# Half 1's convolution with one chunk on TensorE and two on VectorE, later casts for half 2, and block 2's loads behind a gate

## The chip, the cores and the metric

The kernel runs on one core of a Trainium2 chip. The metric is the device time of one execution in microseconds. The kernel before takes 698.72 us (median of three runs, 698.67 to 698.84); its profiled execution has a span of 696.4 us.

## The reference

The input x has 8 sequences of 4096 positions and 192 channels. A causal convolution of 7 taps runs along each sequence; the taps are a softmax over a small weight table, one row for each of 8 heads of 24 channels. Its output goes through two matrix products with a leaky ReLU between them. Cut to what matters:

```python
w = softmax(weight, axis=-1)                      # 8 heads x 7 taps
x_pad = concatenate([zeros(6), x], axis=1)
y[b, s, h, :] = sum_k w[h, k] * x_pad[b, s + k, h, :]
h = y.reshape(32768, 192) @ w_in                  # 192 x 2048
g = maximum(0.01 * h, h)
out = g @ w_out                                   # 2048 x 192, float32
```

## The kernel before

**Tiling.** The 192 channels are cut in three chunks of 64 (NCH, CH). Two sequences are handled together, one on each half of the 128 partitions; four such pairs of 4096 positions make 32 blocks of 512 positions. The first five blocks are handled as two halves of 256 positions each, the others whole. A half or a whole block is a "group"; group 0 is half 0 (block 0, first half), group 1 half 1, group 2 half 2 (block 1, first half), group 4 the first half of block 2. For the first two blocks the text also counts quarters of input q = 0 to 3, one for each of groups 0 to 3.

**Way of the data.** For the first two blocks x is loaded in float32 by SyncE (load_first), cast to bf16 (cast_first, line 128), transposed by TensorE into two PSUM tiles "ptr" (transpose_first, line 143) and copied into xt (evac_first, line 157). From block 2 on, GpSimd loads x with the cast in the transfer (load_x, line 79) and SyncE transposes it by DMA (transpose_x, line 94). The convolution reads xt and writes yt. On VectorE a chunk is seven operations (conv_jobs, one of line 176 and six of line 182). In the opening, some chunks are done on TensorE instead, as 28 matmuls with diagonal weights in a high and a low part (pe_conv_jobs, line 201), whose sum "acc" in PSUM is scaled into yt (line 207, or line 317 on ScalarE).

**The two products.** A step mm1 computes 12 (for a half) or 6 (for a whole block) matmuls into a "ph" tile and one ScalarE activation that writes g (lines 356 and 363). The second product is cut in slots: slot q does one matmul of output q // 16 on the upper 64 rows and, LAG = 24 slots later, one on the lower 64 rows (line 376). An output is copied out of PSUM when its last lower matmul is done (evac_o, line 415), and every second one starts a store (line 418). Half 0 has no slots, as nothing is ready yet; in half 1 there are 16 slots after each of its four pairs of steps.

**Order.** Everything is issued in the written order on each engine; semaphores follow from the tiles. The main loop goes over groups i, pairs of steps j, and steps u. While group i is in the products, VectorE does the convolution of group i + 1 (the list "ahead", handed out in portions after each j). Two PSUM pools matter: "ph" with two tiles of two banks, and "po" with four slots that serve the second product's outputs, the transposed tiles "ptr" (two at a time) and "acc". A slot is free when the last reader of its tile is done.

**The opening.** TensorE runs a few dummy matmuls on zeros (warm) between its first real ones. Half 0's convolution does chunks 0 and 1 on TensorE (NPEC = 2) and chunk 2 on VectorE. In half 0's loop (i == 0), after u = 1, quarter 1 is transposed and evacuated; half 1's convolution does chunk 2 on VectorE, chunk 0 on TensorE after u = 3 and chunk 1 after u = 5. Quarter 2 is cast by ScalarE after u = 2, transposed after u = 4 and evacuated at j = 3, after which VectorE does four of half 2's 21 operations before the rest of them in half 1's loop. Quarter 3 is cast in half 1's loop after u = 0 and u = 2, transposed after j = 1, and evacuated after j = 3, behind the remaining operations of half 2. Block 2's loads and DMA transposes (lines 333 and 334) are issued ahead of the main loop.

Of the kernel before, what the change touches and what calls it, by code (L numbers as in the profile page):

```python
# [9 lines left out]
FP32 = mybir.dt.float32  # L10
# [4 lines left out]
def kernel(  # L15
# [54 lines left out]
    def load_x(blk):  # L70

        if blk >= NBLK:
            return
        rp, st = divmod(blk, NB)
        t = xb_pool.tile([128, NCH, SUB, 2, CH], BF16, name="x_bf")
        src = x[:, st * ST : (st + 1) * ST, :].rearrange("r (s p) d -> r p s d", p=128)
        for c in range(NCH):
            for e in range(2):
                nc.gpsimd.dma_start(  # L79
                    out=t[:, c, :, e, :],  # L80
                    in_=src[2 * rp + e, :, :, c * CH : (c + 1) * CH],
                )
        x_bf[blk] = t

    def transpose_x(blk):

        if blk >= NBLK:
            return
        rp, st = divmod(blk, NB)
        if st == 0:  # L90
            new_xt(rp)
        t = x_bf.pop(blk)
        for c in range(NCH):
            nc.sync.dma_start_transpose(
                out=xt[rp][:, c, HALO + st * ST : HALO + (st + 1) * ST].rearrange(
                    "p (s k) -> p s k", s=SUB
                ),
                in_=t[:, c, :, :, :].rearrange("p s e k -> p (s e k)"),
            )
# [24 lines left out]
    def cast_first(q, e, copy):  # L124
        if q % 2 == 0 and e == 0:
            x_bf[q // 2] = xb_pool.tile([128, NCH, SUB, 2, CH], BF16, name="x_bf")
        h = q % 2
        copy(  # L128
            out=x_bf[q // 2][:, :, h * HS : (h + 1) * HS, e, :],
            in_=x_nat[q][:, e, :, :].rearrange("p s (c k) -> p c s k", c=NCH),  # L130
        )
# [3 lines left out]
    def transpose_first(q):  # L135
        ts = [
            psum_o.tile([128, HS, NCH, CH], BF16, name=f"ptr{i}", tag="po") for i in range(2)
        ]
        for s in range(HS):
            for c in range(NCH):  # L140
                for i in range(2):
                    ps = slice(i * CH, (i + 1) * CH)
                    nc.tensor.transpose(  # L143
                        out=ts[i][:, s, c, :],
                        in_=x_bf[q // 2][ps, c, (q % 2) * HS + s, :, :].rearrange(
                            "p e k -> p (e k)"
                        ),
                        identity=ident[ps, ps],
                    )
        ptr[q] = ts  # L150
# [11 lines left out]
    def conv_jobs(grp, chunks=range(NCH)):  # L162
        blk, t0, T = grp
        rp, st = divmod(blk, NB)
        if blk not in yt:
            yt[blk] = yt_pool.tile([128, NCH, ST], BF16, name="yt")
        y = yt[blk]
        jobs = []
        for c in chunks:
            for k in range(K):  # L170
                a = BASE + k + st * ST + t0
                src = xt[rp][:, c, a : a + T]
                dst = y[:, c, t0 : t0 + T]
                if k == 0:
                    jobs.append(
                        lambda s=src, d=dst, c=c: nc.vector.tensor_scalar_mul(  # L176
                            d, s, wk[:, c, 0:1]
                        )
                    )
                else:  # L180
                    jobs.append(
                        lambda s=src, d=dst, c=c, k=k: nc.vector.scalar_tensor_tensor(  # L182
                            out=d, in0=s, scalar=wk[:, c, k : k + 1], in1=d,
                            op0=mybir.AluOpType.mult, op1=mybir.AluOpType.add,
                        )
                    )
        return jobs

    def pe_conv_jobs(grp, c):


        blk, t0, T = grp
        acc = psum_o.tile([128, ST], FP32, name="acc", tag="po")
        jobs = []
        for p in range(2):
            for k in range(K):
                a = BASE + k + blk * ST + t0
                for e in range(2):
                    ps = slice(e * CH, (e + 1) * CH)
                    jobs.append(  # L200
                        lambda k=k, p=p, a=a, e=e, ps=ps: nc.tensor.matmul(  # L201
                            out=acc[ps, :T], lhsT=diag[c][ps, p, k, :],
                            rhs=xt[0][ps, c, a : a + T],
                            start=(k == 0 and p == 0), stop=(k == K - 1 and p == 1),
                        )
                    )
        return jobs, lambda scale: scale(yt[blk][:, c, t0 : t0 + T], acc[:, :T], rsum[:, c, :])
# [40 lines left out]
    def warm(n):  # L248
        for _ in range(n):
            nc.tensor.matmul(  # L250
                out=wa[:, 0, 0:HT], lhsT=zero[:, 0:128], rhs=zero, start=True, stop=True
            )
# [9 lines left out]
        out=w9[:, 0:K], in_=w9[:, 0:K], func=mybir.ActivationFunctionType.Exp,  # L262
        bias=nmax, scale=1.0, accum_out=w9[:, K : K + 1],
    )
    warm(7)
    wps = psum_h.tile([128, 2, ST], FP32, name="wps", tag="ph")
    for c in range(NCH):
        nc.tensor.matmul(  # L268
# [7 lines left out]
    cast_first(0, 1, nc.scalar.copy)  # L276

    wraw = wps[:, 0, 0 : NCH * (K + 1)].rearrange("p (c k) -> p c k", c=NCH)
    wkh = const_pool.tile([128, NCH, K], BF16, name="wkh")
    wkl = const_pool.tile([128, NCH, K], FP32, name="wkl")  # L280
    nc.vector.tensor_copy(out=wkh, in_=wraw[:, :, 0:K])
    nc.vector.tensor_sub(wkl, wraw[:, :, 0:K], wkh)


    diag = [const_pool.tile([128, 2, K, CH], BF16, name=f"diag{c}") for c in range(NPEC)]
# [14 lines left out]
        return act  # L300

    transpose_first(0)
    warm(3)
    diag_high(0)
    diag_low(0, range(2))
    evac_first(0, nc.vector.tensor_copy, nc.scalar.copy)
# [23 lines left out]
    cast_first(1, 0, nc.vector.tensor_copy)  # L330
    cast_first(1, 1, nc.vector.tensor_copy)
    load_first(3)
    load_x(2)
    transpose_x(2)


    g, po, osb, seal = {}, {}, {}, {}
# [70 lines left out]
    def evac_o(n):  # L408
# [7 lines left out]
        if n % 2 == 1:  # L416
# [3 lines left out]
                in_=osb.pop(n // 2),  # L420
            )

    slot, avail = 0, 0
    for i, grp in enumerate(groups):
        blk, t0, T = grp
        steps = T // 64
        if t0 == 0:
            g[blk] = g_pool.tile([128, NFC, 2, ST], BF16, name="g", tag="g")
        quota = (avail - slot) // steps

        if i == 0:
            ahead, pe_ahead = [], []
        elif i == 1:
            ahead = early[4:]
        else:
            ahead = conv_jobs(groups[i + 1]) if i + 1 < len(groups) else []
        per = -(-len(ahead) // (steps - 1)) if T == ST else -(-len(ahead) // steps)
        for j in range(steps):
            for u in range(2 * j, 2 * j + 2):
                mm1(grp, u)  # L440
                if i == 0 and u == 1:
                    transpose_first(1)
                    evac_first(1, nc.vector.tensor_copy, nc.vector.tensor_copy)
                    ahead = conv_jobs(groups[1], range(NPEC, NCH))
                    evacs = []
                    for c in range(NPEC):
                        pe_jobs, evac_y = pe_conv_jobs(groups[1], c)
                        pe_ahead += pe_jobs
                        evacs.append(evac_y)
                    per = len(ahead)  # L450
                if i == 0 and u == 2:
                    for e in range(2):
                        cast_first(2, e, nc.scalar.copy)
                if i == 0 and u == 4:
                    transpose_first(2)
                    evacs[0](act_scale)
                if i == 0 and u in (3, 5):
                    for job in pe_ahead[: 4 * K]:
                        job()
                    pe_ahead = pe_ahead[4 * K :]  # L460
                if i == 1 and u in (0, 2):
                    cast_first(3, u // 2, nc.scalar.copy)
            for _ in range(quota):
                mm2_slot(slot)
                slot += 1
            if i == 0 and j == 3:
                evac_first(2, nc.vector.tensor_copy, nc.vector.tensor_copy)
                early = conv_jobs(groups[2])
                for job in early[:4]:
                    job()  # L470
                evacs[1](nc.vector.tensor_scalar_mul)
            for job in ahead[per * j : per * (j + 1)]:
                job()
            if i == 1 and j == 1:
                transpose_first(3)
            if i == 1 and j == 3:
                evac_first(3, nc.vector.tensor_copy, nc.vector.tensor_copy)

            last_half = t0 + T == ST
            if j == steps // 4 and last_half:  # L480
                load_x(blk + 3)
            if j == steps // 2 and last_half and blk > 0:
                transpose_x(blk + 2)
        avail += 2 * T // 128 * NFC
# [37 lines left out]
```

## Time and profile before

| | busy, us | share of span |
|---|---|---|
| TensorE matmul (PE) | 689.5 | 99% |
| TensorE weight load (PEld) | 612.7 | 88% |
| VectorE (DVE) | 538.2 | 77% |
| ScalarE (ACT) | 513.3 | 74% |
| GpSimd (POOL) | 142.1 | 20% |

| group of instructions | count | busy, us | mean, ns |
|---|---|---|---|
| L356 PE, first product | 3552 | 391.8 | 347 |
| L376 PE, second product | 8048 | 398.1 | 243 |
| L363 ACT, activation | 512 | 496.5 | 1021 |
| L182 DVE, convolution | 642 | 439.7 | 685 |
| L201 PE, convolution | 112 | 7.3 | 280 |
| L157 DVE, evacuation of a transposed tile | 7 | 2.2 | 352 |

Matmuls overlap, so the mean duration of one is not the time from one to the next. In a line of the timeline the first number is the start in microseconds from the beginning of the span, the second the time from the start of the first to the end of the last instruction merged into the line, then engine, source line, operation, tile written, tiles read, and the count; brackets give the idle time of the engine just before and what ended it. A few matmul records can be missing.

In the first 60 us a group of 21 convolution operations on halves takes VectorE some 10 us (chunks start at 30.14, 33.48, 36.86 and 40.18), and a half in both products takes TensorE 10.5 us.

### The profile page before, as it was taken

The numbers are of one execution on the slowest core, as the hardware profiler recorded it, in microseconds if no ns is written. First come the engines' busy times: TensorE is split into PE (matmuls) and PEld (weight loads), VectorE is DVE, ScalarE is ACT, GpSimd is POOL, SyncE is SP. The second block draws the span as 40 slices with busy tenths as digits, with TensorE's granted clock in tenths as the row PEclk, the third lists the DMA queues.
The fourth block names the chain that finished last, engine by engine and source line by source line (L and its number), as shares of the span: only waits on it lengthen the run. The fifth ranks groups of instructions, "written<-read, shape, count | busy, mean of one in ns | idle before, by whom it ended". The sixth has DMA issues, their size and how long they took to land.

```text
span 696.4 us, 26058 instructions
## 1 busy us (share of the span) xinstructions
PE 689.5 (99%) x11786; PEld 612.7 (88%) x11786; DVE 538.2 (77%) x991; ACT 513.3 (74%) x579; POOL 142.1 (20%) x198
## 2 busy tenths in 40 slices
PE   8999999999999999999999999999999999999997
PEld 6899999678888888888888888888888888888887
DVE  6899999768777788777787777787777787777712
ACT  6888888977777777777777777777777777777770
POOL 6342221320122220222220222211222220000000
PEclk9999999999999999999999999999999999999999
DMA  9986553853556545556545556645556644122112
GB/s 173 127 98 76 82 80 77 88 78 73 76 65 92 82 70 81 74 66 93 81 69 81 73 69 93 79 67 85 66 76 88 86 71 72 53 52 59 47 37 69
DMA packets 184847, 54.39 MB, mean 78 GB/s; under 512 B 148384, under 2 KB 184736, under 8 KB 184736
## 3 DMA queue, kind: packets, MB, share of 16 engines
q0 software_dynamic: 98768, 14.17, 29.7%
q1 hardware_dynamic: 85968, 38.56, 23.1%
q8 instruction: 92, 1.51, 0.9%
q14 instruction: 19, 0.16, 0.1%
HBM read 29.88 MB, written 25.17 MB: 79 GB/s over the span
## 4 chain that ended last, share of the span: by engine, by line
PE 97%; DMA 1%; ACT 1%; POOL 0%; issue 0%; DVE 0%; SPq 0%; POOLq 0%; ACTq 0%
PE po L376 49%; PE ph L356 47%; DMA x_nat<-in_x_dram 1%; ACT g L363 1%; PE acc L201 0%; PE wps L268 0%; ACT diag L296 0%; POOL sel L228 0%; PE warm L250 0%; PE ptr L143 0%; ACT x_bf L128 0%; ACT xt L157 0%; POOL sel L226 0%; DVE o_sb L415 0%; POOL ident masks.py:199 0%
## 5 line engine op out<-in xcount | busy, mean ns | idle before, releaser
L363 ACT ACTIVATE g<-ph 128x1024 bf16<-128x1024 f32 x512 | 496.5, 1021 | 161.0 <-PE ph L356 161.0
L182 DVE SCALAR_TENSOR_TENSOR yt<-xt,wk,yt 128x512 bf16<-128x512 bf16 (+1 forms) x642 | 439.7, 685 | 17.4
L376 PE MATMUL po<-w_out,g 64*128 64x192 bf16 (+1 forms) x8048 | 398.1, 243 | 0.1
L376 PEld LDWEIGHTS <-g 64*128 64x128 bf16 (+1 forms) x8048 | 372.2, 94 | 28.8 <-ACT g L363 0.4
L356 PE MATMUL ph<-yt,w_in 64*128 64x512 bf16 (+1 forms) x3552 | 391.8, 347 | 1.6 <-ACT g L363 1.3
L356 PEld LDWEIGHTS <-w_in 64*128 64x128 bf16 x3552 | 249.9, 94 | 46.1 <-issue 5.0
L79 POOL DMA_DIRECT2D x_bf<-in_x_dram x180 | 133.7, 773 | 431.0 <-DMA xt<-x_bf 422.9
L415 DVE COPY o_sb<-po 128x192 f32<-128x192 f32 x216 | 77.2, 358 | 129.5 <-PE po L376 127.2
L176 DVE TENSOR_SCALAR yt<-xt,wk 128x512 bf16<-128x512 bf16 (+1 forms) x107 | 35.9, 336 | 1.0 <-DMA xt<-x_bf 0.8
L415 ACT COPY o_sb<-po 128x192 f32<-128x192 f32 x40 | 13.1, 327 | 0.0
L201 PE MATMUL acc<-xt,diag 64*64 64x256 bf16 x112 | 7.3, 280 | 0.0
L201 PEld LDWEIGHTS <-diag 64*64 64x64 bf16 x112 | 6.0, 111 | 1.2 <-issue 0.6
L250 PE MATMUL warm<-zero 128*128 128x256 bf16 x20 | 4.5, 373 | 1.1 <-DVE junk L218 1.1
L128 ACT CAST x_bf<-x_nat 128x384 bf16<-128x384 f32 x5 | 2.5, 507 | 3.6 <-DMA x_nat<-in_x_dram 3.6
L238 POOL DMA_DIRECT2D w_in<-in_moe_w_in_dram x8 | 5.1, 643 | 0.0
L157 DVE COPY xt<-ptr 128x384 bf16<-128x384 bf16 x7 | 2.2, 352 | 2.8 <-PE ptr L143 2.8
L250 PEld LDWEIGHTS <-zero 128*128 128x128 bf16 x20 | 2.0, 122 | 2.2 <-DVE junk L218 1.1
L296 ACT ACTIVATE diag<-ident,wkl 128x64 bf16<-128x64 bf16 x14 | 3.6, 339 | 0.0
L128 DVE CAST x_bf<-x_nat 128x384 bf16<-128x384 f32 x3 | 1.2, 439 | 1.4 <-DMA x_nat<-in_x_dram 1.4
L317 ACT ACTIVATE yt<-acc,rsum 128x256 bf16<-128x256 f32 x3 | 1.4, 470 | 1.2 <-PE acc L201 1.2
L143 PEld LDWEIGHTS <-x_bf 64*128 64x128 bf16 x48 | 1.2, 101 | 1.0 <-ACT x_bf L128 1.0
L268 PEld LDWEIGHTS wps<-w,sel 8*128 8x128 f32 x6 | 1.4, 322 | 0.7 <-POOL sel L228 0.7
(28 smaller groups left out, 12.5 us busy)
## 6 DMA issues: line engine op xcount, KB each, us to landing
out_dram<-o_sb SPq DMA_DIRECT2D x128, 192.0 KB, 2.1
x_bf<-in_x_dram POOLq DMA_DIRECT2D x180, 64.0 KB, 3.3
x_nat<-in_x_dram SPq DMA_DIRECT2D x8, 192.0 KB, 5.8
w_in<-in_moe_w_in_dram POOLq DMA_DIRECT2D x8, 192.0 KB, 7.8
xt<-x_bf SPq DMA_TRANSPOSE x90, 2.5
w_out<-in_moe_w_out_dram POOLq DMA_DIRECT2D x1, 768.0 KB, 14.2
w<-in_weight_dram SPq DMA_DIRECT2D x1, 0.2 KB
```

What stands on the lines that cost most here:

```text
L79: nc.gpsimd.dma_start(out=t[:, c, :, e, :], in_=src[2 * rp + e, :, :, c * CH : (c + 1) * CH],)
L128: copy(out=x_bf[q // 2][:, :, h * HS : (h + 1) * HS, e, :], in_=x_nat[q][:, e, :, :].rearrange("p s (c k) -> p c s k", c=NCH),)
L176: lambda s=src, d=dst, c=c: nc.vector.tensor_scalar_mul(d, s, wk[:, c, 0:1])
L182: lambda s=src, d=dst, c=c, k=k: nc.vector.scalar_tensor_tensor(out=d, in0=s, scalar=wk[:, c, k : k + 1], in1=d, op0=mybir.AluOpType.mult, ...
L201: lambda k=k, p=p, a=a, e=e, ps=ps: nc.tensor.matmul(out=acc[ps, :T], lhsT=diag[c][ps, p, k, :], rhs=xt[0][ps, c, a : a + T], start=(k == ...
L238: nc.gpsimd.dma_start(out=w_in[e * CH : (e + 1) * CH, :, fs], in_=moe_w_in[:, fs].rearrange("(c p) f -> p c f", p=CH),)
L250: nc.tensor.matmul(out=wa[:, 0, 0:HT], lhsT=zero[:, 0:128], rhs=zero, start=True, stop=True)
L296: act = nc.scalar.activation(out=diag[c][:, 1, k, :], in_=ident2, func=mybir.ActivationFunctionType.Copy, scale=wkl[:, c, k : k + 1],)
L356: nc.tensor.matmul(out=ph[:, e, i * T : (i + 1) * T], lhsT=w_in[ps, c, f * 128 : (f + 1) * 128], rhs=y[ps, c, t0 : t0 + T], start=(c == 0) ...
L363: act = nc.scalar.activation(out=g[blk][:, nf * u : nf * (u + 1), :, t0 : t0 + T], in_=ph.rearrange("p e (i t) -> p i e t", i=nf), func=my ...
L376: ins = nc.tensor.matmul(out=po[m], lhsT=g[b][ps, fc, e, s * 128 : (s + 1) * 128], rhs=w_out[ps, fc, :], start=(rt != 1 and fc == 0), stop ...
L415: copy(out=o_sb[:, n % 2, :], in_=po.pop(n))
```

## The change

The change rearranges the opening. Half 1's convolution keeps only chunk 0 on TensorE and gives chunks 1 and 2 to VectorE, which removes 28 matmuls and one ScalarE evacuation there. Half 2's casts move from after u = 2 to after u = 5 and u = 6, so that ScalarE doesn't stand in front of a load that has not landed; its transposes and evacuation follow at the end of half 0, and none of half 2's convolution is done ahead. Block 2's loads move into half 1's loop behind a copy of one element on GpSimd that reads half 0's last activation; they leave the DMA engines to the weights and to quarters 2 and 3 until then. Block 2's DMA transposes move into half 2's loop. Three more dummy matmuls are run, and the tables wkh and wkl hold only the two chunks that TensorE uses.

```diff
-    warm(7)
+    warm(9)
...
-    wkh = const_pool.tile([128, NCH, K], BF16, name="wkh")
-    wkl = const_pool.tile([128, NCH, K], FP32, name="wkl")
-    nc.vector.tensor_copy(out=wkh, in_=wraw[:, :, 0:K])
-    nc.vector.tensor_sub(wkl, wraw[:, :, 0:K], wkh)
+    wkh = const_pool.tile([128, NPEC, K], BF16, name="wkh")
+    wkl = const_pool.tile([128, NPEC, K], FP32, name="wkl")
+    nc.vector.tensor_copy(out=wkh, in_=wraw[:, 0:NPEC, 0:K])
+    nc.vector.tensor_sub(wkl, wraw[:, 0:NPEC, 0:K], wkh)
...
     transpose_first(0)
-    warm(3)
+    warm(4)
...
     load_first(3)
-    load_x(2)
-    transpose_x(2)
...
+    pjunk = const_pool.tile([1, 1], BF16)
     slot, avail = 0, 0
...
         if i == 0:
-            ahead, pe_ahead = [], []
-        elif i == 1:
-            ahead = early[4:]
+            ahead = []
...
                 if i == 0 and u == 1:
                     transpose_first(1)
                     evac_first(1, nc.vector.tensor_copy, nc.vector.tensor_copy)
-                    ahead = conv_jobs(groups[1], range(NPEC, NCH))
-                    evacs = []
-                    for c in range(NPEC):
-                        pe_jobs, evac_y = pe_conv_jobs(groups[1], c)
-                        pe_ahead += pe_jobs
-                        evacs.append(evac_y)
+                    pe_ahead, evac_y = pe_conv_jobs(groups[1], 0)
+                    ahead = conv_jobs(groups[1], range(1, NCH))
                     per = len(ahead)
-                if i == 0 and u == 2:
-                    for e in range(2):
-                        cast_first(2, e, nc.scalar.copy)
-                if i == 0 and u == 4:
-                    transpose_first(2)
-                    evacs[0](act_scale)
-                if i == 0 and u in (3, 5):
-                    for job in pe_ahead[: 4 * K]:
+                if i == 0 and u == 3:
+                    for job in pe_ahead:
                         job()
-                    pe_ahead = pe_ahead[4 * K :]
+                if i == 0 and u in (5, 6):
+                    cast_first(2, u - 5, nc.scalar.copy)
...
             if i == 0 and j == 3:
+                evac_y(nc.vector.tensor_scalar_mul)
+                transpose_first(2)
                 evac_first(2, nc.vector.tensor_copy, nc.vector.tensor_copy)
-                early = conv_jobs(groups[2])
-                for job in early[:4]:
-                    job()
-                evacs[1](nc.vector.tensor_scalar_mul)
+            if i == 1 and j == 1:
+
+                nc.gpsimd.tensor_copy(out=pjunk, in_=g[0][0:1, NFC - 1, 1, HT - 1 : HT])
+                load_x(2)
+            if i == 2 and j == 1:
+                transpose_x(2)
             for job in ahead[per * j : per * (j + 1)]:
                 job()
```

## The prediction

> **What bounds the kernel now.** I read the engine table first, then the chain that ended last, then the timeline of the first 36 us. In the page:
>
> ```profile
> PE 689.5 (99%) x11786; PEld 612.7 (88%) x11786; DVE 538.2 (77%) x991; ACT 513.3 (74%) x579; POOL 142.1 (20%) x198
> ...
> PE 97%; DMA 1%; ACT 1%; POOL 0%; issue 0%; DVE 0%; SPq 0%; POOLq 0%; ACTq 0%
> ```
>
> TensorE is 97% of the chain. From about 25 us on it never stops: the stages 25 to 30, 30 to 35 and so on each show 5.00 us of PE in 5.00. So the time is the opening, until TensorE runs dense, plus a fixed amount of dense matmul. A change in the opening moves the end by the same number of microseconds, if nothing opens a new hole later. Whether it does is the whole question, so I follow the opening on three engines. ScalarE in the first half (timeline; start, duration, engine, line):
>
> ```profile
> 14.93 0.50 ACT L128 CAST x_bf<-x_nat 128x384 bf16<-128x384 f32 x1
> 17.00 0.51 ACT L128 CAST x_bf<-x_nat 128x384 bf16<-128x384 f32 x1 [1.57 <-DMA x_nat<-in_x_dram]
> 17.42 1.93 ACT L363 ACTIVATE g<-ph 128x1024 bf16<-128x1024 f32 x2
> 19.23 0.48 ACT L317 ACTIVATE yt<-acc,rsum 128x256 bf16<-128x256 f32 x1
> 19.59 1.03 ACT L363 ACTIVATE g<-ph 128x1024 bf16<-128x1024 f32 x1
> 21.77 2.96 ACT L363 ACTIVATE g<-ph 128x1024 bf16<-128x1024 f32 x3 [1.15 <-PE ph L356]
> ```
>
> The second cast of quarter 2 waits 1.57 us for its load, and every activation behind it waits too; later ScalarE waits 1.15 us behind the second convolution on TensorE. Those two holes are what the change goes after. Now VectorE and TensorE, same timeline:
>
> ```profile
> 17.95 0.62 DVE L157 COPY xt<-ptr 128x384 bf16<-128x384 bf16 x2 [1.00 <-PE ptr L143]
> ...
> 18.61 0.29 DVE L176 TENSOR_SCALAR yt<-xt,wk 128x256 bf16<-128x256 bf16 x1
> ...
> 29.50 0.61 DVE L157 COPY xt<-ptr 128x384 bf16<-128x384 bf16 x2
> ...
> 29.90 1.50 PE L376 MATMUL po<-w_out,g 64*128 64x192 bf16 x32
> ```
>
> VectorE evacuates quarter 2 at 17.95, starts half 2's convolution at 18.61 and ends it just before 29.50, where it evacuates quarter 3. TensorE's next second-product matmuls begin at 29.90. That is no coincidence. The "po" pool has four slots. In half 1 the slots hold outputs 0 and 1 (neither finished: output 0's second row tile runs only from slot 24 to 39 of the output order) and the two transposed tiles of quarter 3. At slot 32 the matmul of output 2 wants a slot, and only the copy at 29.50 can give it one. TensorE is in order, so everything behind slot 32 waits. Today the copy (345 to 358 ns) is done at 29.85 and the matmul starts at 29.90: it fits with nothing to spare.
>
> **What the Trainium skill says.** "PSUM — Partial Sum Buffer", Specifications (TRN2): eight banks of 2 KiB per partition. The two "ph" tiles take two banks each and the four "po" slots one each, so all eight are in use and there is no fifth slot. "PSUM — Partial Sum Buffer", Engine vs sequencer instructions: VectorE and ScalarE are strict FIFO and matmuls start in program order; the trace agrees (1.57 us of ScalarE idle behind one late cast). "TensorE: Matmul & The Clock Gate", What's actually happening: after one idle window of about 3.4 us the array falls to half rate until a busy window has passed. The trace shows the slow rate only at the start (three warm matmuls take 0.82 us at 5.78 and 0.50 us at 8.58); it has no later idle gap of that length.
>
> **The change, part by part.**
>
> Opening warm-ups, 9 for 7 and 4 for 3. The first seven span 1.13 to 2.80, so 0.21 to 0.24 us each; nine would end near 3.2, where the weights' matmuls now start at 3.00 (+0.05 to +0.25 on those, whose results VectorE uses at 4.48, while the path waits for ScalarE's cast until 5.25). The fourth one before the first convolution ends near 6.6 instead of 6.4, and that convolution starts at 6.52: +0.1. Against it, the clock may rise earlier: the first convolution takes 2.13 us where a warm one takes 1.72, so at most 0.4 to win. I take 0, ends -0.4 and +0.3.
>
> Chunk 1 of half 1 moves off TensorE. It removes 28 matmuls, 1.72 us (19.25 to 20.97), and one ScalarE evacuation (0.48). It adds 7 operations on VectorE: a chunk takes 3.35 us from start to start (30.14, 33.48, 36.86, 40.18). VectorE then runs 14 operations from 13.54 to 20.24, and chunk 0's evacuation (0.4) to 20.65. It is idle today from 16.95 to 17.95, and from 18.61 on it does four operations of half 2 ahead of time; that early start is lost.
>
> Quarter 2's casts move behind activations 5 and 6. ScalarE takes 0.97 us from one activation to the next (1.94 for two, 2.96 for three) and 0.43 from a cast to the next operation (17.00 to 17.42): activations 0 to 3 run from 12.07 to 16.0. The one convolution (14.82 to 16.54) holds the fourth until its 12 matmuls (0.83) end at 17.3. Then 4 at 17.33, 5 at 18.3, cast at 19.25, 6 at 19.65, cast 20.6 to 21.1, 7 from 21.0 to 22.05. Loads for this are there by 17.0 even today. TensorE waits for the cast, transposes at 21.15, and half 1 begins at about 21.5 where it now begins at 22.85. **TensorE is 1.3 us ahead here.**
>
> Half 2's convolution. The transposed quarter 2 reaches VectorE at 21.15 plus the 0.44 that lies today between the end of the cast (17.51) and the copy (17.95): 21.6. Copies 0.66, so the convolution starts at 22.25. Its 21 operations, three chunks, take 10.04, to 32.3. Then quarter 3's first copy, 0.35: done at 32.65. The edit leaves the transposes of quarter 3 and their evacuation where they were in program order, after all 21. **Output 2's first matmul so starts at about 32.7 and not 29.90**, while TensorE is ready for it at about 28.4 (from 21.5: the same work that takes 22.85 to 30.0 today, without the 0.5 that it waits for activations). A hole of some 4.3 us opens; the 1.3 us and all other gain ahead of it vanish in it. From there TensorE's work is the same as today: **32.7 - 29.9 = +2.8 us**. VectorE alone sets a floor: 13.54 + 6.7 + 0.4 + 0.66 + 10.04 + 0.35 = 31.7 with no idle at all, which is +1.8.
>
> Block 2's loads behind the gate. GpSimd copies one element after half 0's last activation (near 22.1), then issues six loads at 0.74 us, so they land near 30. The copy's cost is not in the trace; the nearest row is a 128x1 memset of 0.1 us, I allow up to 1. Behind it queue these loads and block 3's, nothing else. What they free is the transfer of w_in, w_out (landed at 23.79) and quarter 2 between 10 and 20 us; the hole on TensorE hides any gain from it. Block 2's transposes now stand on the SyncE queue behind half 0's outputs (the second pair is ready at 39.5 today, so about 42.3), and land 2.5 to 4.5 us later. VectorE wants them at 32.65 + 0.3 + 10.04 = 43.0 and waits 2 to 4 us; it then ends half 4's convolution at 55 to 57, and TensorE needs it at 54.9 + 2.8 = 57.7. Hidden, narrowly: 0, at worst +1.
>
> Smaller constants (two chunks for three in the high and low tables): the same operations on fewer columns, nothing.
>
> Sum: 698.72 + 2.8 + 0 = 701.5 us.
>
> **Rivals.** *Half-rate clock after the hole.* A 4.3 us hole is longer than the page's 3.4 us window, but the window is not aligned to it. If the clock falls, the next 3.4 us or so of matmul run at half rate and lose half of that, 1.7 us, and more if it takes two windows: 703.2 to 704.9. For it: the length. Against it: only a hole that holds a whole window counts. Chance 0.22. *The slot wait does not bind* (the copy finds its way ahead, or the slot comes from elsewhere): TensorE then keeps the 1.3 us, half 2 needs its convolution at 33.85 - 1.3 = 32.55 against 32.3, and the time is 697.4. For it: TensorE's 1.72 us really goes. Against it: the count of four slots, and today's 29.85 beside 29.90. Chance 0.07. *Between*, a warm clock 0.4 us sooner and ScalarE less held up, VectorE near its floor: +1.2, 699.9. Chance 0.07. Forecast, +2.8: 0.64.
>
> **Range and chances.** The forecast's unknowns (warm-ups -0.4 to +0.3, casts +-0.4, late transposes up to +1) give 700.4 to 702.8; the upper part of the clock case reaches 704. I take 700.3 to 704.0. Slower by over 0.2% means above 700.1: forecast and clock case, 0.86. Within 0.2% (697.3 to 700.1): the case between and part of the rival that keeps the gain, 0.09. Faster: 0.05.
>
> **What would show it.** TensorE idle for 4 us just before the "po" matmuls near 32.7, released by VectorE's copies of line 157; those copies some 3 us later than 29.50; half 1's first matmul near 21.5 and no wait of ScalarE for quarter 2's load; VectorE waiting 2 to 4 us for block 2's transposes near 43; slower matmuls for some 3 us after the hole only in the clock case. Wrong, if output 2 starts before quarter 3's copies, or if those copies come before half 2's convolution has ended.

## The result and the profile after

The changed kernel takes 704.96 us (median of four runs, 704.79 to 705.34) against 698.78 us for the kernel before on the same chip (four runs, 698.67 to 699.05): ratio 1.0089, 95% interval 1.0071 to 1.0106. It is 6.2 us slower where 2.8 us were forecast, and outside the range. A second measurement on another chip, told below, gave 705.95 us and 1.0102 (1.0087 to 1.0118).

The two lines of the page that answer to those shown of before, engine table and chain:

```profile
PE 691.3 (98%) x11761; PEld 613.6 (87%) x11761; DVE 541.8 (77%) x998; ACT 513.2 (73%) x578; POOL 142.2 (20%) x199
...
PE 85%; DVE 12%; ACT 1%; issue 1%; DMA 1%; SPq 0%; ACTq 0%
```

In the chain 12% now lies on VectorE, where it was 0%. That is some 84 us, in two stretches: 22.1 to 33.8 us and 50.1 to 125.1 us. TensorE runs 25 matmuls fewer (28 gone, three dummies more) and is busy 1.8 us longer: some of its matmuls became slower. For the first stretch the list of waits for TensorE says (engine, line waited for: total us, times, longest):

```profile
PE po L374 <- DVE xt L157: 4.8, 1, 4.8
```

It is one single wait. The second stretch is taken up below. The timeline around the wait (the file is eight lines shorter, so the first product is now L354, the second L374, the activation L361):

```profile
21.10 0.52 ACT L128 CAST x_bf<-x_nat 128x384 bf16<-128x384 f32 x1
...
22.06 0.62 DVE L157 COPY xt<-ptr 128x384 bf16<-128x384 bf16 x2 [0.78 <-PE ptr L143]
...
22.71 0.29 DVE L176 TENSOR_SCALAR yt<-xt,wk 128x256 bf16<-128x256 bf16 x1
...
26.04 0.58 DVE L176 TENSOR_SCALAR yt<-xt,wk 128x256 bf16<-128x256 bf16 x1
...
27.44 1.49 PE L354 MATMUL ph<-yt,w_in 64*128 64x256 bf16 x24
...
29.66 0.66 DVE L176 TENSOR_SCALAR yt<-xt,wk 128x256 bf16<-128x256 bf16 x1
...
33.36 0.61 DVE L157 COPY xt<-ptr 128x384 bf16<-128x384 bf16 x2
33.77 2.58 PE L374 MATMUL po<-w_out,g 64*128 64x192 bf16 x30 [4.84 <-DVE xt L157]
```

TensorE ends its first-product matmuls at 28.93 and stands until 33.77, when the first of quarter 3's copies has freed a slot. Then 30 second-product matmuls take 2.58 us, where 32 took 1.50 in the kernel before. The table by stages shows why. Columns: stage; its length; busy time (and count) of PE, PEld, DVE, ACT, POOL; granted TensorE clock; DMA share; GB/s.

```profile
28.90:33.70 4.80, 0.03 (x2) 0.00 (x0) 4.55 (x11) 1.36 (x2) 4.80 (x7) 0.84 1.44 93
33.70:36.20 2.50, 2.44 (x32) 2.43 (x33) 2.32 (x7) 0.32 (x1) 2.50 (x4) 0.50 1.40 89
36.20:38.80 2.60, 2.60 (x28) 2.18 (x26) 2.42 (x7) 0.97 (x1) 0.01 (x1) 0.50 0.88 56
38.80:41.50 2.70, 2.70 (x60) 2.66 (x57) 2.52 (x7) 1.69 (x4) 0.00 (x0) 0.97 0.11 32
```

The clock falls to 0.50 while the array is idle and stays there until about 39.0, so 5.2 us of matmul run at half rate. Half 2's first product starts at 40.23; in the kernel before it starts at 33.85. The difference, 6.4 us, is nearly the whole of what the two profiles differ by: their spans are 696.4 and 703.0 us. (That is 6.6 us and not 6.2, as the profiled execution of the kernel before took 698.09 us, less than any of the four runs above.)

The last 0.3 us belong to the second stretch of the chain. Near 44 us VectorE runs out of input, and 80 us later TensorE meets what that cost it. From the list of VectorE's waits, and from the chain in order of time (start, length, what):

```profile
DVE yt L176 <- DMA xt<-x_bf: 6.0, 1, 6.0
...
124.27 0.76 DVE yt L182
125.08 1.04 PE ph L354 x8
```

VectorE waits 6.0 us for block 2's late transposes, starts again at 50.06 and then works without a pause until the first whole block's convolution is done, just before 125.08, where TensorE takes up its last chunk. TensorE's list shows no wait there, but from the first product's first 12 matmuls of this block to the next 12 it now takes 2.21 us (124.39 to 126.60), where it took 1.95 (118.01 to 119.96).

### The profile page after: what moved, and what is told of

Read it like the earlier page. It is cut to its first block, busy times and chain, and to the rows that moved or that the text cites. A ratio compares the mean times of both kernels' runs of the same rounds, so it can differ in the third digit from the quotient of the medians.

```text
span 703.0 us, 26013 instructions
## 1 busy us (share of the span) xinstructions
PE 691.3 (98%) x11761; PEld 613.6 (87%) x11761; DVE 541.8 (77%) x998; ACT 513.2 (73%) x578; POOL 142.2 (20%) x199
## 4 chain that ended last, share of the span: by engine, by line
PE 85%; DVE 12%; ACT 1%; issue 1%; DMA 1%; SPq 0%; ACTq 0%
PE po L374 42%; PE ph L354 41%; DVE yt L182 11%; ACT g L361 1%; DVE yt L176 1%; PE acc L201 1%; PE warm L250 1%; DMA xt<-x_bf 1%; PE wps L268 0%; DVE xt L157 0%; PE ptr L143 0%; ACT x_bf L128 0%; SPq L416 0%; DVE o_sb L413 0%; ACT o_sb L413 0%
## 5 line engine op out<-in xcount | busy, mean ns | idle before, releaser
L361 ACT ACTIVATE g<-ph 128x1024 bf16<-128x1024 f32 x512 | 496.7, 1021 | 163.9 <-PE ph L354 163.8
L374 PE MATMUL po<-w_out,g 64*128 64x192 bf16 (+1 forms) x8048 | 399.6, 243 | 5.0 <-DVE xt L157 4.8
L374 PEld LDWEIGHTS <-g 64*128 64x128 bf16 (+1 forms) x8048 | 373.6, 94 | 34.1 <-issue 5.2
L354 PE MATMUL ph<-yt,w_in 64*128 64x512 bf16 (+1 forms) x3552 | 393.3, 348 | 1.0 <-ACT g L361 0.7
L354 PEld LDWEIGHTS <-w_in 64*128 64x128 bf16 x3552 | 250.9, 94 | 46.0 <-issue 3.8
L201 PE MATMUL acc<-xt,diag 64*64 64x256 bf16 x84 | 5.8, 292 | 0.0
L143 PE MATMUL ptr<-ident,x_bf 64*128 64x64 bf16 x48 | 1.6, 202 | 0.9 <-ACT x_bf L128 0.9
```

The source lines that it names most:

```text
L201: lambda k=k, p=p, a=a, e=e, ps=ps: nc.tensor.matmul(out=acc[ps, :T], lhsT=diag[c][ps, p, k, :], rhs=xt[0][ps, c, a : a + T], start=(k == ...
L354: nc.tensor.matmul(out=ph[:, e, i * T : (i + 1) * T], lhsT=w_in[ps, c, f * 128 : (f + 1) * 128], rhs=y[ps, c, t0 : t0 + T], start=(c == 0) ...
L361: act = nc.scalar.activation(out=g[blk][:, nf * u : nf * (u + 1), :, t0 : t0 + T], in_=ph.rearrange("p e (i t) -> p i e t", i=nf), func=my ...
L374: ins = nc.tensor.matmul(out=po[m], lhsT=g[b][ps, fc, e, s * 128 : (s + 1) * 128], rhs=w_out[ps, fc, :], start=(rt != 1 and fc == 0), stop ...
```

## The experiments

The theory after the result: output 2 waits for a PSUM slot, the slot for quarter 3's copies, the copies for VectorE's 21 operations, and the clock falls in the hole. The rivals: the added VectorE work costs of itself wherever the copies stand; the slow stretch has another cause than the idle array; the gate or the dummy matmuls are to blame. "Before" in each ratio is the kernel before, run beside it on the same chip: 698.63 us for the first four, 698.65 for the next four, 698.77 for the last three.

**Copies early.** The changed kernel, with quarter 3's copies directly behind its transposes.

```diff
             if i == 1 and j == 1:
                 transpose_first(3)
-            if i == 1 and j == 3:
                 evac_first(3, nc.vector.tensor_copy, nc.vector.tensor_copy)
```

> The changed kernel, with quarter 3's two evacuations issued right behind its transposes (after j = 1 of half 1), ahead of the last nine operations of half 2's convolution. If output 2's slot is what TensorE waits for: VectorE is at the copies at about 28.5 us, output 2's matmul starts at about 29.0 instead of 33.8, the clock stays up, and half 2's first product waits for its convolution, which ends at about 33.4 plus 0.6, so it starts at about 34 instead of 40.2: some 6 us less than the changed kernel, 698.5 to 699.3. If the extra work on VectorE itself is the cost, and not the place of the copies, TensorE waits for half 2's convolution just as long and the time stays above 702.

699.26 us, ratio 1.0006 (0.9998 to 1.0014): the loss is gone, with all other edits of the change still in. Its timeline at the same place:

```profile
29.17 0.61 DVE L157 COPY xt<-ptr 128x384 bf16<-128x384 bf16 x2
29.57 1.50 PE L374 MATMUL po<-w_out,g 64*128 64x192 bf16 x32 [0.18 <-DVE xt L157]
...
33.52 0.40 PE L354 MATMUL ph<-yt,w_in 64*128 64x256 bf16 x4
```

The wait shrinks from 4.84 to 0.18 us, the 32 matmuls take 1.50 us again, and half 2 starts at 33.52. The place of the copies in VectorE's order, and not the amount of its work, makes the hole. That this kernel is still no faster than before, although half 2 starts 0.3 us sooner in its profile, has a second wait in its list:

```profile
PE ph L354 <- DVE yt L182: 1.2, 2, 1.0
```

The wait of 1.0 lies between 114 and 120 us, where the kernel goes from halves to whole blocks. VectorE works 14.5 us on a whole block's convolution (18 operations of 749 ns and three of 351, from the groups of the kernel before kept apart by shape) while TensorE does the last half in 10.5 us; what is missing must come from VectorE's lead, and this kernel has used its lead up.

**The hole filled.** Dummy matmuls on zeros in the hole, in the changed kernel; no result uses them. First 38, then 31.

```diff
+            if i == 1 and j == 2:
+                wb = psum_h.tile([128, 2, ST], FP32, name="wb", tag="ph")
+                for _ in range(38):
+                    nc.tensor.matmul(
+                        out=wb[:, 0, 0:HT], lhsT=zero[:, 0:128], rhs=zero,
+                        start=True, stop=True,
+                    )
             for _ in range(quota):
```

> The changed kernel with 38 dummy matmuls on zeros put ahead of slot 32 in half 1, in the place where TensorE stands idle (about 4.1 us of them at full rate; no result uses them). If the idle array lost its clock and that cost 2.5 us: output 2 still starts near 33.8, its 32 matmuls take 1.5 us instead of 2.6, and the time is 702.3 to 702.8. If the slow stretch after the hole has another cause (late weights, the activations), nothing or a slowdown: 704.9 or more.

703.58 us (702.96 to 705.53), ratio 1.0073 (1.0060 to 1.0086), above what was expected: in its profile the dummies end at 35.48, while the copies start at 34.40, so they fill the hole and 0.65 us more. For a clean comparison the count was cut to 31, and the changed kernel was run unedited beside it:

> The changed kernel once more, unedited, on the chip on which the next three run. The hole on TensorE and the slow stretch behind it as before, 704.5 to 705.3. If the slow stretch depends on where the hole falls against a window of the clock gate, single runs spread by 1 to 3 us, from about 702 (hole alone) to 705.3.

> The changed kernel with 31 dummy matmuls ahead of slot 32 instead of 38, which in the run with 38 ended 0.65 us after the slot was free (no result uses them). If the clock costs some 2 us: full rate behind the hole, 702.3 to 703.0, and single runs closer together than those of the changed kernel. If filling the hole only traded one loss for another: as with 38, 703.6.

705.95 us (ratio 1.0102, 1.0087 to 1.0118) unedited, somewhat above what was expected, and 702.72 us (1.0052, 1.0040 to 1.0065) filled. Idle time turned into useless work makes the kernel 3.2 us faster. Stages of the filled kernel:

```profile
29.00:34.00 5.00, 4.54 (x70) 4.05 (x65) 4.71 (x10) 2.63 (x3) 5.00 (x8) 1.00 1.40 90
34.00:36.00 2.00, 1.86 (x35) 1.62 (x34) 1.86 (x7) 0.21 (x1) 2.00 (x4) 1.00 1.47 93
36.00:39.00 3.00, 3.00 (x70) 3.00 (x67) 2.82 (x7) 2.00 (x4) 1.33 (x2) 1.00 1.35 88
```

The clock is 1.00 all through, output 2 starts at 34.91 and half 2 at 38.86: 3.95 us, as in the kernel before (29.90 to 33.85), against 6.46 in the changed kernel (33.77 to 40.23). So the clock's share is 2.5 us there. The second profile of the unedited kernel, which is of its slowest execution (707.38 us), also has a wait of 1.5 us of TensorE for VectorE's yt at 127.7 us. It is the place at which the first profile loses 0.3 us; the filled kernel loses nothing there. So the 3.2 us may hold some of both.

**The dummy matmuls of the opening.** The kernel before with 9 for 7 and 4 for 3.

```diff
-    warm(7)
+    warm(9)
...
-    warm(3)
+    warm(4)
```

> The kernel before with the three added dummy matmuls alone (9 for 7, 4 for 3). If the dummy matmuls delay the opening: half 0's first product starts at 11.7 instead of 11.1 and the time is 0.3 to 0.6 us longer, 699.1 to 699.4 (part of it may be hidden behind the load of quarter 2). If they are hidden or bring the clock up sooner: 698.4 to 698.8.

698.88 us, ratio 1.0005 (0.9996 to 1.0013): between the two expectations, and no difference is shown. The profiles say more than the time. Half 0's first product starts between 11.72 and 12.87 (mean 12.3) in the eight profiles with the added dummies and between 11.11 and 12.36 (mean 11.7) in the five without. Most of this difference is not the dummies' doing. Each trace's record of the clock begins with its first rise to full rate, and that lies anywhere from 7.39 to 10.82 us. (The matmuls agree: the first convolution on TensorE, which would take 1.72 us at full rate, takes 2.13 with the rise at 7.39 and 2.36 with the rise at 8.26.) In the five profiles without the dummies the first product follows the rise: 11.11 for a rise at 7.39, 12.36 for one at 10.07, and the three others within 0.03 us of the straight line through these two. The eight with the dummies lie 0.16 to 0.28 us above that line, this run 0.21. So the dummies cost 0.2 us, and the rest is when the clock happened to rise. Whether they also move the rise is not shown: 8.26 to 10.82 with them and 7.39 to 10.07 without.

**The gate.** The changed kernel with block 2's loads and transposes back ahead of the main loop.

```diff
     load_first(3)
+    load_x(2)
+    transpose_x(2)
...
-            if i == 1 and j == 1:
-
-                nc.gpsimd.tensor_copy(out=pjunk, in_=g[0][0:1, NFC - 1, 1, HT - 1 : HT])
-                load_x(2)
-            if i == 2 and j == 1:
-                transpose_x(2)
```

> The changed kernel with block 2's loads and transposes put back ahead of the main loop, without the gate. If the gate is no part of the loss: the hole and the slow clock stay. VectorE's two slow first operations in half 2's convolution (0.58 and 0.66 us for 0.29) lie in the stretch where GpSimd issues 18 loads in a row; if those cause it, they fall back to 0.3 and the time is 0.6 us shorter, 704.3; VectorE's wait of 6.0 us near 50 goes, and costs nothing either way. If the gate caused the loss, the time falls to 700 or less.

703.07 us (701.51 to 703.98), ratio 1.0060 (1.0047 to 1.0073). The hole and the slow clock stay, so the gate did not make them. But without it the kernel is 0.3 to 0.4% less slow, 2 to 3 us, and not 0.6. Three parts are seen in the profile. VectorE's convolution of half 2 takes 9.97 us (23.35 to 33.32) and not 10.65, as its first operations of a chunk fall back to 0.28 us. VectorE is no longer late at the first whole block: the step that took 2.21 us in the changed kernel takes 1.95 again. And the clock is back 3.0 us after the hole instead of 5.2; this part need not be the gate's, as the slow clock comes and goes between executions of this one kernel (last section). How much each part is worth is not settled.

**Late casts or moved chunk.** Two kernels part these. First the changed kernel, with quarter 2's casts in the stretch where ScalarE waits for the convolution:

```diff
-                if i == 0 and u in (5, 6):
-                    cast_first(2, u - 5, nc.scalar.copy)
+                if i == 0 and u == 3:
+                    for e in range(2):
+                        cast_first(2, e, nc.scalar.copy)
+                if i == 0 and u == 4:
+                    transpose_first(2)
...
                 evac_y(nc.vector.tensor_scalar_mul)
-                transpose_first(2)
```

> The changed kernel with quarter 2's casts both after u = 3, where ScalarE waits 1.4 us for the convolution on TensorE, and its transposes after u = 4. If VectorE's 14 operations of half 1 set when half 2's convolution starts, and not the late casts: quarter 2 waits for VectorE, VectorE loses only its idle 0.8 us at 21.3, output 2's matmul starts 0.8 us sooner at 33.0, TensorE arrives up to 1 us sooner, so the hole gets no shorter: 703.8 to 704.4. If the late casts are the cause: the hole all but goes, 700 or less.

702.94 us (701.01 to 704.35), ratio 1.0050 (1.0032 to 1.0067), less than expected. Counted from half 0's first product, output 2 comes 1.45 us sooner (20.60 for 22.05), 0.87 of it from VectorE's idle time and the rest from its first operations, less slowed; TensorE arrives at the same point as before (17.2), since it now waits for chunk 0's scaling and for w_out. The hole of 3.4 us still brings the clock down in this profile, for 3.4 us. Most of the loss is still there with early casts. Second, the kernel before, with the moved chunk alone:

```diff
-                    ahead = conv_jobs(groups[1], range(NPEC, NCH))
+                    ahead = conv_jobs(groups[1], range(1, NCH))
                     evacs = []
-                    for c in range(NPEC):
+                    for c in range(1):
...
-                evacs[1](nc.vector.tensor_scalar_mul)
```

> The kernel before with chunk 1 of half 1 on VectorE as its only edit: casts, transposes, loads and dummy matmuls as before, and the four operations of half 2 still issued ahead of time. VectorE starts half 2's convolution near 20.9 instead of 18.6, and the copies come near 31.3, so output 2 starts 1.5 us later than before while TensorE arrives about 1 us earlier. If the moved chunk is enough to make the hole: 2.5 us of hole and 700.0 to 700.5, with the clock up as the hole is short; 702 or more if it falls all the same. If the loss needs the late casts: 698.7 or less.

701.09 us (700.03 to 702.59), ratio 1.0040 (1.0028 to 1.0052). The chunk by itself costs 2.3 us in the median, and both expectations for it came true: three executions took 700.03 to 700.88 us with a mean granted clock of 1.000, and three took 701.30 to 702.59 us with 0.997 or 0.998. The profile is of the first kind. Its waits of TensorE:

```profile
PE po L376 <- DVE xt L157: 1.2, 1, 1.2
PE po L376 <- DMA w_out<-in_moe_w_out_dram: 1.1, 1, 1.1
```

Output 2 starts at 31.97, 2.1 us later than before, and the copies again release it. TensorE came early enough for a larger hole, but spent 1.1 us of it waiting for w_out first. In this profile the clock stays at 1.00; no profile shows the other three executions.

**Was the slot the bound already?** The kernel before with its casts after u = 3; with that and quarter 3's copies inside half 2's convolution; and with both and the gate.

```diff
-                if i == 0 and u == 2:
+                if i == 0 and u == 3:
                     for e in range(2):
                         cast_first(2, e, nc.scalar.copy)
...
-            for job in ahead[per * j : per * (j + 1)]:
+            for n, job in enumerate(ahead[per * j : per * (j + 1)]):
                 job()
+                if i == 1 and j == 2 and n == 2:
+                    evac_first(3, nc.vector.tensor_copy, nc.vector.tensor_copy)
...
-            if i == 1 and j == 3:
-                evac_first(3, nc.vector.tensor_copy, nc.vector.tensor_copy)
```

> The kernel before with the casts of quarter 2 after u = 3 as its only edit; quarter 3's evacuation stays behind all of half 2's operations. If VectorE's copies are what output 2's matmul waits for already today: whatever TensorE gains ahead of them is given back there, 698.4 to 698.7. If not: the gain of the run with both moves, 697.9.

> The kernel before with two moves: quarter 2's casts after u = 3 instead of u = 2, so that activation 3 does not stand behind a load, and quarter 3's evacuation inside half 2's convolution, after three of the operations of j = 2. Both chunks of half 1 stay on TensorE. ScalarE's wait of 1.57 us goes, half 1's first product starts about 1.2 us sooner (21.6), and the slot of output 2 is free by 28.5, so nothing gives it back: 697.4 to 697.8. If the copies stay the bound, or ScalarE only moves its wait: 698.5 or more.

> The kernel of the run before (kernel before, casts of quarter 2 after u = 3, quarter 3's evacuation inside half 2's convolution) with block 2's loads behind the gate on GpSimd and block 2's transposes after j = 2 of half 1, ahead of half 0's stores. If the gate frees transfers for quarter 2: ScalarE's last wait for it, 0.99 us, shrinks to 0.3 and the time falls by 0.4 to 0.7 us, 697.2 to 697.5. If the transposes come late again or the loads slow VectorE: no gain, 697.9 or more.

Casts alone: 698.55 us, 0.9997 (0.9990 to 1.0005), no difference, and TensorE waits 0.27 us for the copies where it had no wait before. Casts and copies: 697.91 us, 0.9991 (0.9984 to 0.9998), faster than the kernel before by 0.7 us, a little less than expected; the list of TensorE's waits behind 24 us is empty in its profile. The gap to the kernel with casts alone is in the direction of the theory, but their intervals overlap. With the gate and early transposes: 698.17 us, 0.9992 (0.9985 to 1.0000), no gain on top. Half 1 starts at 22.33 there and not at 22.75, but TensorE then waits 0.28 us for w_out, and output 2 starts at 29.77, as without the gate (29.73). So in this profile, with the slot free in time, the landing of w_out near 24 us is what TensorE meets next.

## Why the prediction was wrong

**What held.** The way of the loss is the one foretold, step by step: the four slots, the copies behind all 21 operations, output 2 as the matmul that waits, TensorE idle for more than 4 us, released by the copies of line 157. Half 1's first product started at 21.86 (forecast 21.5), and the transposes of block 2 made VectorE wait near 50 (6.0 us, where 2 to 4 were forecast). The rival "slot wait does not bind" is out, by the run with early copies.

**The sum, term by term, on half 2's start (33.85 before, 40.23 after):**

| term | forecast | measured |
|---|---|---|
| output 2 late, as worked out | +2.8 | +2.8 |
| half 0's first product later | 0 | +0.6 (0.2 from the dummies, 0.4 from the clock's later rise, 8.26 for 7.39), less 0.15 regained |
| VectorE's 21 operations | 10.04 us | 10.65 us: +0.6 |
| clock after the hole | 0 in the forecast (rival: 1.7, or 3.4 with two windows) | +2.5 |
| sum | +2.8 | +6.4 |

**The step that failed** is the clock's term. The forecast put it at 0 and left it to a rival with a chance of 0.22, on the argument that only a hole that holds a whole window counts, which a hole of 4.3 us would seldom do. The traces say otherwise: in all four profiled kernels with a hole of 3.4 to 4.8 us the clock fell, 2.7 to 3.7 us after TensorE's last matmul. A window did not have to be empty: before three of the four falls it held matmuls for 6, 8 and 20% of its length (last section). By the mean granted clock it fell in all eight executions of the changed kernel. So a forecast that itself opens a hole of 4.3 us should have had the slow clock in its main case. The Trainium skill, "TensorE: Matmul & The Clock Gate", What's actually happening, gives a window of about 3.4 us, and the traces agree with its length (3.41); the fault was the discount on it. The rival's size was fair: 1.7 us, or 3.4 with two windows, where 2.5 were measured, and its range, 703.2 to 704.9, misses the measured 704.96 by little. But the range that was stated took in this rival only up to 704.0.

**Two smaller terms** went the same way. The opening was set at 0 with ends -0.4 and +0.3, and the profile shows +0.6 at half 0's first product; 0.4 of that is the luck of the two profiled executions and no cost of the change. VectorE's convolution was put at 10.04 us, from the stretch 30.14 to 40.18, and took 10.65. GpSimd issues loads in that stretch too (from 33.05), but there two first operations of a chunk took 0.34 and 0.33 us, and behind the gate two took 0.58 and 0.66. These two moved the wait to 33.8, and with the clock's 2.5 us they carried the time over the range's upper end.

**Late transposes** were called hidden, narrowly, because TensorE would need half 4 only at 57.7. There they are hidden. But VectorE did not win its lead over TensorE back, and at the first whole block it was gone: 0.3 us lost near 125 in the first profile, and a wait of 1.5 us at 127.7 in the second one of the same kernel. The prediction did not look that far.

**Two sums** of the prediction are off by little. TensorE's arrival, 21.5 plus 7.15 less 0.5, is 28.15 and not 28.4; but the wait of 0.5 lies ahead of the work that was counted, so it was not to be taken off: the work took 7.07 us (21.86 to 28.93). And its unknowns, added up, give 700.7 to 703.2 and not 700.4 to 702.8.

## What to carry to other kernels

When work moves to an in-order engine, look not only at what it computes but at the copies that stand behind it: here 7 operations more and 4 fewer ahead of time kept a 0.35 us copy from freeing a PSUM slot, and moving the copy alone took back 5.7 us. If a change is expected to leave TensorE idle for some 3 us or more, the slow clock behind the hole belongs in the main case; below that it may still come in some executions, as with the moved chunk. And an engine's lead is stock for a later stage: the wait near 44 us was paid near 125. Such a debt shows in the chain before it shows as a wait.

## What the runs showed of the hardware that was not expected

**The clock works in windows of 3.41 us that run from its first rise.** The record of the clock in four traces, with the share of matmul (from its records, whose ends are modelled) in the window that ended with the fall and in the windows at half rate:

| kernel | first rise, us | hole | fell | back | matmul in the window before the fall | in the slow windows |
|---|---|---|---|---|---|---|
| changed | 8.26 | 28.93 to 33.77 | 32.15 | 38.98 | 0.06 | 0.53, 1.00 |
| changed, again | 9.69 | 30.85 to 34.85 | 33.58 | 40.41 | 0.20 | 0.63, 1.00 |
| loads at once | 9.44 | 29.80 to 33.72 | 33.33 | 36.75 | 0.00 | 0.89 |
| casts in the gap | 9.08 | 29.29 to 32.72 | 32.98 | 36.39 | 0.08 | 1.00 |

The edge of the first fall, by stages (columns as above):

```profile
31.90:32.15 0.25, 0.00 (x0) 0.00 (x0) 0.23 (x1) 0.00 (x0) 0.25 (x1) 1.00 1.22 78
32.15:32.40 0.25, 0.00 (x0) 0.00 (x0) 0.25 (x1) 0.00 (x0) 0.25 (x2) 0.50 1.62 103
```

All four falls come 23.89 us after the rise, seven times 3.413, and the clock stays down for 3.41 or 6.83 us, one window or two. It also falls in every trace at the end of the kernel, again at the edge of a window. Over all 13 traces, windows with up to 27% of matmul brought it down and none with 48% or more did. It came back after a window with 89 or 100%, and not after one with 53 or 63%. What lies between is not measured. As the rise moves between 7.39 and 10.82 us, the same hole meets the windows differently from one execution to the next.

The mean granted clock that is listed for every execution fits this: one slow window in 703 us makes 0.998, two make 0.995, and the end of the kernel can take off up to 0.001 more. By that count the changed kernel had two slow windows in seven of its eight executions and one in the other. The kernel with its loads at once had none at 701.5 us, one at 702.4 and 703.1, two at 703.8 and 704.0. The one with casts in the gap had none at 701.0 and 701.4, and one in the four executions from 702.8 to 704.4. With the hole filled by 31 dummies there was none in five, 702.3 to 703.1.

**A VectorE operation takes longer while GpSimd issues loads.** The convolution's first operation of a chunk takes 0.28 to 0.29 us, but 0.58 and 0.66 in the changed kernel at 26.04 and 29.66, amid GpSimd's 18 loads (22.84 to 36.2), and 0.28 there without the gate. Not each one is hit: at 34.01, amid the same loads, it took 0.29. In the 13 profiles there are 346 such operations on halves. None of the 229 that run beside no load instruction of GpSimd took over 0.32 us; of the 117 that do, 47 took 0.32 to 0.67. The six that follow it take 0.485 us in either. Why some are hit and others not is open.
